# Loading the second expert's weights after the main loop instead of inside it

## The chip, the core and the metric

The kernel runs on one core of a Trainium2 chip. A core has five engines that take their instructions in order, each from its own stream: TensorE (PE, matrix products; its weight loads are listed as PEld), VectorE (DVE), ScalarE (ACT), GpSimd (POOL) and SyncE (SP, which here issues most DMAs). Sixteen DMA engines move data between the main memory (HBM) and the core's on-chip memory (SBUF); PE writes to a small accumulator memory (PSUM). The metric is the device time of one execution in microseconds (us), given as the median of several runs.

## What is computed

Three layers follow each other: masked attention, a dense layer with a softplus, and a mixture of eight experts in which each token takes at most one expert.

```python
# attention: q, k, v are (4, 8, 576, 64); keys of later blocks of 64 are masked
scores = np.where(mask, scale * q @ k.T, -1e9)
attn = exp(scores - max) / (sum(exp) + 1e-9);  x = (attn @ v) as (2304, 512)
# dense layer, 512 -> 2048 -> 512, in float32
h = x @ w_in;  x = softplus(h) @ w_out
# mixture of experts, E = 8, 512 -> 1024 -> 512
do_compute = x @ w_skip > 0;  out = x.copy()
xc = x[do_compute]
e_idx = argmax(xc @ w_gate, axis=1);  gate_w = softmax(xc @ w_gate)[e_idx]
for e in range(E):
    mask = e_idx == e
    if mask.any():
        y[mask] = gate_w[mask, None] * (relu(xc[mask] @ w1[e]) @ w2[e])
out[do_compute] = xc + y
```

One expert has two weight matrices of 2 MB each (w1: 512 x 1024, w2: 1024 x 512, float32). Which experts are needed, and for which tokens, is only known once the dense layer has produced those tokens.

## The kernel before

**Main loop.** After the attention, a loop of 80 steps (and 2 to drain) computes the dense layer. The 2304 tokens are cut into five chunks, numbered 0 to 4 here: four of 512 tokens and a last one of 256. The loop goes through the hidden columns in four groups and inside each group through the chunks, so that in the last group the chunks become final one after the other. Step `s` holds `layer1` (L570), `softplus` (L581 to L591) and, two steps late, `layer2` (L622). When a chunk is final, `close_unit` adds up its tiles (DVE, L633) and SP stores each tile twice: to a scratch copy `xd`, from which expert rows are gathered later, and to the output (L641).

**Routing, step by step beside the loop.** For each finished chunk, `transpose_x2`, `logits`, `route` and `append` find each token's expert and its place in that expert's list. The results `si` and `pay` are ready with the reciprocal of L746 on DVE; then `scatter` (L753) has POOL write them to the lists `lst` in HBM, 128 tokens in each scatter. A chunk of 512 tokens takes four scatters, the last chunk two. Each scatter waits until the scatter before it has landed, since they all write `lst`.

**Expert order.** After chunk 1, `rank_experts` ranks the experts by the number of tokens seen so far; the number of the largest (rank 0, the first expert) and of the next (rank 1, the second expert) are read by SP from a small table `tab` (`value_load`, L907). After chunk 2 the rest are ranked. `load_expert(r, b, part)` (L904 to L917) issues an expert's weights as eight DMAs of 512 KB on SP: parts 0 to 3 are w1 (L910), parts 4 to 7 are w2 (L915). They go to pages that the dense layer has finished with. SP's DMAs use eight semaphores in turn, so that each of them first waits for the landing of the one that stands eight before it.

**Early tiles.** For ranks 0 and 1 the first 128 listed tokens of chunks 0 to 2 are computed early: `early_lists` loads the two lists (L920, `idxe`) after the scatters of chunk 2; `early_rows` gathers the tokens' rows from `xd` (POOL, L923); `early_turn` transposes them (PE, L949; copy on DVE, L951); `early_l1` and `early_l2` (L964, L976) are the two products. The calls stand in the code behind the loop, woven with the routing of the last chunk.

**The rest.** The tokens that are left, here few for each of ranks 0 to 2, are computed together in `side_by_side`. Its rows come over the same path: lists complete (last scatter), `late_rows` loads the list pieces (L1000, `idxf`), gathers the rows (L923, `xgf`), `turn` transposes them (L1035), and then come L1576, L1587, L1600, L1610 and the last store (L928). In PE's order the transposes of L1035 stand in front of the last quarter of the second expert's early product.

The order of everything above is written out in the program. Steps of the routing are put at loop steps by `later(c, n, ...)`: n steps after the step in which chunk c is computed for the last time.

Of the kernel before, what the change touches and what calls it, by code (L numbers as in the profile page):

```python
# [22 lines left out]
def attention_softplus_moe_kernel(  # L23
# [13 lines left out]
    nc = tc.nc  # L37
# [3 lines left out]
    E, _, F = w1.shape  # L41
# [24 lines left out]
    tab = const.tile([1, 4, E], I32, name="tab")  # L66
    MAXF = (NT - 2 * P) // P
    further = const.tile([1, 3, MAXF], I32, name="further")
# [587 lines left out]
    def logits(c, t):  # L656

        if t == 0:
            lgs[c] = ps_r.tile([P, 512], F32, tag="lg", name="lg")
        if c >= last - 1 and t % 2:  # L660
            ps = ps_r.tile([P, P], F32, tag="tr", name="lq")
        else:
            ps = lgs[c][:, 256 + t % 2 * P:256 + (t % 2 + 1) * P]
        xt = x2T.pop((c, t))
        for kc in range(KC):
            nc.tensor.matmul(
                out=ps[32 * kc:32 * (kc + 1), :], lhsT=wg[:, kc, :], rhs=xt[:, kc, :], start=True, stop=True,
                tile_position=(0, 32 * kc),
            )
        lq = x2T[c, t] = rt_p.tile([P, P], F32, tag="lq", name="lq")  # L670
        nc.scalar.activation(out=lq, in_=ps, func=AF.Copy)
# [209 lines left out]
    def expert_page(b, j):  # L881

        if (b, j) not in pages:
            i = j - KC
            pages[b, j] = (
                x_page((0, 2, 3)[b], j) if i < 0 else x_page(1, i) if b == 0 else slot(2 * b + i // 2, "io"[i % 2])
            )
        return pages[b, j]

    def expert_w1(b, kc, f):  # L890

        return expert_page(b, kc).rearrange("p h c -> p (h c)")[:, f]
# [8 lines left out]
    NPART = KC + KF // 2  # L901
    expert_at = {}

    def load_expert(r, b, part):  # L904

        if part == 0 and r != "further":
            expert_at[r] = nc.sync.value_load(tab[0:1, int(r > 1), r:r + 1], min_val=0, max_val=E - 1)  # L907
        e = bass.ds(expert_at[r], 1)
        if part < KC:
            nc.sync.dma_start(  # L910
                out=expert_w1(b, part, slice(0, F)), in_=w1[e, part * P:(part + 1) * P, :].rearrange("o p f -> p (o f)")
            )
            return
        kf = 2 * (part - KC)
        nc.sync.dma_start(  # L915
            out=expert_page(b, part), in_=w2[e, kf * P:(kf + 2) * P, :].rearrange("o (h p) d -> p (o h) d", p=P)
        )  # L917

    def load_list(idx, s0):
        nc.sync.dma_start(out=idx, in_=lst[bass.ds(s0, P), :])  # L920
# [12 lines left out]
    early = {}  # L933

    def early_lists(a):
        idx = const.tile([P, 2], I32, name=f"idxe{a}")
        load_list(idx, expert_at[a] * STRIDE)
        early[a] = [idx]
# [16 lines left out]
    def early_l1(a, quarter):  # L955
        xgT, hT = early[a][2:4]
        half, odd = divmod(quarter, 2)
        if not odd:
            early[a, "pf"] = ps_h.tile([P, KF // 2, P], F32, tag="h", name="pfe")
        pf = early[a, "pf"]  # L960
        for f in range(odd * KF // 4, (odd + 1) * KF // 4):
            ff = half * (KF // 2) + f
            for kc in range(KC):
                nc.tensor.matmul(  # L964
                    out=pf[:, f, :], lhsT=expert_w1(a, kc, slice(ff * P, (ff + 1) * P)), rhs=xgT[:, kc, :],
                    start=(kc == 0), stop=(kc == KC - 1),
                )
        if odd:
            nc.scalar.activation(out=hT[:, half * (KF // 2):(half + 1) * (KF // 2), :], in_=pf, func=AF.Relu)
# [17 lines left out]
    def later(c, n, do, *args):  # L987

        routing_work.setdefault(after[c] + n, []).append(lambda: do(*args))
# [164 lines left out]
    later(1, 5, rank_experts)  # L1154
    for i in range(NPART):
        later(1, 6 + i // 4, load_expert, 0, 0, i)
        later(1, 8 + i // 4, load_expert, 1, 1, i)
    later(2, 5, rank_experts, True)
    later(2, 5, list_starts)
    for a in range(2):  # L1160
        later(2, 6, early_lists, a)
        later(2, 7, early_rows, a)
# [248 lines left out]
    for kc in range(KC):  # L1411
        for c, of in enumerate((X0, X1)):
            a, b = of[2 * kc], of[2 * kc + 1]
# [72 lines left out]
    for t in range(nt):  # L1486
        transpose_x2(last, t)
    early_l1(0, 1)
    for i in range(NPART):
        load_expert(2, 2, i)  # L1490
    logits(last, 0)
    early_l1(0, 2)
    logits(last, 1)
# [190 lines left out]
```

## Time and profile before

| | |
|---|---|
| time, median of 3 runs | 715.69 us (714.16 to 717.24) |
| the profiled execution's own time | 716.66 us |
| its span, first to last instruction | 714.9 us |
| PE busy | 681.4 us (95%) |
| DVE, ACT, POOL busy | 478.7, 369.1, 163.7 us |
| DMA | 57.78 MB, mean 81 GB/s |

PE is busy for 95% of the span, but the share says nothing of a single stage. The page's strip of 40 slices (17.9 us each) shows where the rest is:

```profile
PE   8999999999999999999999999999999999986996
PEclk9999999999999999999999999999999999997999
DMA  7536344342210111011011010100003041984520
GB/s 177 126 81 152 85 103 100 85 110 70 62 51 29 43 46 39 22 59 60 30 34 54 30 60 30 59 30 31 0 1 118 2 118 48 348 299 138 214 77 10
```

Each digit is a share in tenths; PEclk is the granted clock of TensorE. The slices 35 and 36 (607 to 643 us) hold the loads of the first two experts, slice 38 (661 to 679 us) that of the third. In slice 37 (643 to 661 us) PE is busy for 6 tenths and its clock is below full.

### The profile page before, as it was taken

To read this page: it belongs to the slowest core of one execution; us is meant where nothing else is said; L and a number is where in the kernel's file an instruction comes from. 1 tells how busy PE (TensorE), PEld (TensorE's weight loads), DVE (VectorE), ACT (ScalarE), POOL (GpSimd) and SP (SyncE) were. 2 spreads that over 40 slices of the span, in tenths; PEclk is the share of its full clock that TensorE was granted. 3 is DMA by queue.
4 is the path that set the end of the run, shared out by engine and by line. 5 is a ranking of instruction groups with operands and counts; after the bars stand their busy time and mean duration, and the time that the engine had idled before them with its cause. 6 is when DMAs were issued, how large, how long until landed. Compare 5 with 4: busy or idle time off the path is not lost. (4 is left out here: it accounts for less than half of the span.)

```text
span 714.9 us, 11536 instructions
## 1 busy us (share of the span) xinstructions
PE 681.4 (95%) x4164; PEld 525.9 (74%) x4164; DVE 478.7 (67%) x951; ACT 369.1 (52%) x884; POOL 163.7 (23%) x180
## 2 busy tenths in 40 slices
PE   8999999999999999999999999999999999986996
PEld 6677676776767888888888888888888777765742
DVE  4787787877898985677656688657765465473322
ACT  4887887878776655455444454444433323220111
POOL 2122121212266452122111122221110021113120
PEclk9999999999999999999999999999999999997999
DMA  7536344342210111011011010100003041984520
GB/s 177 126 81 152 85 103 100 85 110 70 62 51 29 43 46 39 22 59 60 30 34 54 30 60 30 59 30 31 0 1 118 2 118 48 348 299 138 214 77 10
DMA packets 88739, 57.78 MB, mean 81 GB/s; under 512 B 67391, under 2 KB 76607, under 8 KB 88674
## 3 DMA queue, kind: packets, MB, share of 16 engines
q1 hardware_dynamic: 86034, 54.40, 26.2%
q0 software_dynamic: 1296, 2.24, 1.1%
q8 instruction: 34, 0.56, 0.3%
q10 hardware_dynamic: 1344, 0.33, 0.2%
q14 instruction: 31, 0.25, 0.1%
HBM read 46.16 MB, written 10.92 MB: 80 GB/s over the span
## 5 line engine op out<-in xcount | busy, mean ns | idle before, releaser
L570 PE MATMUL h<-xs,wi 128*128 128x512 f32 (+1 forms) x960 | 215.6, 373 | 0.4 <-DVE xs L551 0.4
L570 PEld LDWEIGHTS h<-xs,wi 128*128 128x128 f32 x960 | 168.6, 188 | 36.7 <-issue 0.8
L622 PE MATMUL o<-wo,gh 128*128 128x512 f32 x576 | 183.0, 398 | 0.3 <-DVE wo L559 0.3
L622 PEld LDWEIGHTS o<-wo,gh 128*128 128x128 f32 x576 | 106.3, 188 | 24.0 <-DVE wo L559 0.8
L585 DVE SCALAR_TENSOR_TENSOR e<-h,e 128x512 f32<-128x512 f32 (+1 forms) x80 | 50.8, 635 | 105.0 <-ACT e L583 104.5
L622 PE MATMUL o<-wo,gl 128*128 128x512 f32 x288 | 114.2, 397 | 0.0
L581 ACT ACTIVATE e<-h 128x512 f32<-128x512 f32 (+1 forms) x80 | 44.1, 551 | 132.9 <-PE h L570 132.9
L268 POOL TENSOR_TENSOR cc<-cc,cb 128x512 f32<-128x512 f32 (+1 forms) x40 | 43.4, 1086 | 262.0 <-DVE cb L266 191.5
L412 ACT ACTIVATE p<-s,mx 128x128 f32<-128x128 f32 (+2 forms) x144 | 79.2, 554 | 35.9 <-DVE mx L394 18.9
L437 PE MATMUL tp<-ident,p 128*128 128x128 f32 x384 | 61.2, 284 | 12.1 <-ACT pt L463 9.1
L591 DVE TENSOR_TENSOR gl<-e,gh 128x512 fp32r<-128x512 f32 (+1 forms) x80 | 64.3, 804 | 6.5
L622 PEld LDWEIGHTS o<-wo,gl 128*128 128x128 f32 x288 | 54.2, 188 | 13.1
L437 PEld LDWEIGHTS tp<-ident,p 128*128 128x128 f32 x384 | 42.3, 141 | 21.4 <-ACT pt L463 13.0
L399 DVE TENSOR_REDUCE mx<-s 128x2 f32<-128x256 f32 (+1 forms) x64 | 50.9, 819 | 10.3 <-PE s L388 9.1
L481 PE MATMUL v<-pt,vr 128*64 128x320 f32 (+4 forms) x448 | 50.3, 364 | 0.0
L590 DVE CAST gh<-e 128x512 fp32r<-128x512 f32 (+1 forms) x80 | 44.2, 553 | 6.7 <-DVE e L585 0.5
L583 ACT ACTIVATE e<-e 128x512 f32<-128x512 f32 (+1 forms) x80 | 47.2, 590 | 2.5
L582 ACT ACTIVATE e<-e 128x512 f32<-128x512 f32 (+1 forms) x80 | 47.2, 589 | 2.5
L753 POOL DMA_INDIRECT lst<-pay,si x18 | 17.7, 985 | 128.6 <-DVE pay L746 80.5
L463 ACT ACTIVATE pt<-tp 128x512 f32<-128x512 f32 (+1 forms) x80 | 44.3, 558 | 3.0 <-PE tp L437 2.2
L481 PEld LDWEIGHTS v<-pt,vr 128*64 128x64 f32 x448 | 29.4, 136 | 20.3 <-issue 5.2
L260 ACT ACTIVATE cc<-raw 128x512 f32<-128x512 uint32 (+1 forms) x40 | 23.1, 578 | 25.6 <-POOL ca L269 25.5
(242 smaller groups left out, 942.5 us busy)
## 6 DMA issues: line engine op xcount, KB each, us to landing
xs<-in_moe_w_dram SPq DMA_DIRECT2D x16, 512.0 KB, 6.6
raw<-in_moe_w_in_dram SPq DMA_DIRECT2D x12, 512.0 KB, 3.7
raw<-in_moe_w_out_dram SPq DMA_DIRECT2D x12, 512.0 KB, 3.2
xd<-xT SPq DMA_DIRECT2D x18, 256.0 KB, 3.4
out_dram<-xT SPq DMA_DIRECT2D x18, 256.0 KB, 4.1
vr<-in_v_dram SPq DMA_DIRECT2D x32, 128.0 KB, 3.2
qr<-in_q_dram SPq DMA_DIRECT2D x30, 128.0 KB, 2.6
kr<-in_k_dram SPq DMA_DIRECT2D x30, 128.0 KB, 2.8
```

What stands on the lines that cost most here:

```text
L399: nc.vector.tensor_reduce(out=mx[:, c:c + 2], in_=ps[:, :, columns(t)], axis=AX.X, op=ALU.max, negate=True)
L412: nc.scalar.activation(out=y, in_=x, func=AF.Exp, bias=mx[:, c:c + 1], accum_out=sums[p][:, 0, 2 * t + h:2 * t + h + 1])
L437: nc.tensor.transpose(ps[:, at:at + P], pn[t, g][:, j * P:(j + 1) * P], ident)
L463: nc.scalar.activation(out=dst, in_=x, func=AF.Copy)
L481: nc.tensor.matmul(out=ps[h * D:(h + 1) * D, c0 - q0:q1 - q0], lhsT=vt[:, kt, h, :], rhs=rhs, start=(kt == 0), stop=(kt == nk - 1), skip_g ...
L570: nc.tensor.matmul(out=ps[:, 0:n], lhsT=a[:, kc, :], rhs=b[:, 0:n], start=(kc == 0 and j == 0), stop=(kc == KC - 1 and j == 2),)
L582: nc.scalar.activation(out=e[:, 0:n], in_=e[:, 0:n], func=AF.Exp, scale=-1.0)
L583: nc.scalar.activation(out=e[:, 0:n], in_=e[:, 0:n], func=AF.Ln, bias=1.0)
L585: nc.vector.scalar_tensor_tensor(out=g[:, 0:n], in0=ps[:, 0:n], scalar=0.0, in1=e[:, 0:n], op0=ALU.max, op1=ALU.add)
L590: nc.vector.tensor_copy(out=gh[:, 0:n], in_=g[:, 0:n])
L591: nc.vector.tensor_tensor(out=gl[:, 0:n], in0=g[:, 0:n], in1=gh[:, 0:n].bitcast(F32), op=ALU.subtract)
L622: nc.tensor.matmul(out=acc[c, t], lhsT=a[:, ts], rhs=b, start=(fc == f0 and j == 0), stop=(fc == f1 - 1 and j == 2),)
```

## The change

The eight loads of the second expert (rank 1) leave the steps at which chunk 3 is finished and go behind the main loop, directly in front of the third expert's. Since `early_lists(1)` still needs that expert's number, it now reads it itself, and `load_expert` does not read it again.

```diff
     def load_expert(r, b, part):
 
-        if part == 0 and r != "further":
+        if part == 0 and r not in expert_at and r != "further":
             expert_at[r] = nc.sync.value_load(tab[0:1, int(r > 1), r:r + 1], min_val=0, max_val=E - 1)
...
     def early_lists(a):
+        if a not in expert_at:
+            expert_at[a] = nc.sync.value_load(tab[0:1, int(a > 1), a:a + 1], min_val=0, max_val=E - 1)
         idx = const.tile([P, 2], I32, name=f"idxe{a}")
         load_list(idx, expert_at[a] * STRIDE)
...
     for i in range(NPART):
         later(1, 6 + i // 4, load_expert, 0, 0, i)
-        later(1, 8 + i // 4, load_expert, 1, 1, i)
...
     early_l1(0, 1)
-    for i in range(NPART):
-        load_expert(2, 2, i)
+    for r in (1, 2):
+        for i in range(NPART):
+            load_expert(r, r, i)
     logits(last, 0)
```

Only SP's stream is reordered; the instructions of PE, DVE, ACT and POOL stand in the same order as before, with line numbers two higher. In SP's stream of before, from the end of the first expert's loads to the lists of the early tiles, w1 of the second expert (`xs_6656` to `xs_6662`) stands ahead of chunk 3's eight stores and its w2 (`wi_6752` to `wo_6758`) behind them:

```order
L907 TENSOR_LOAD tab_65
...
L910 DMA xs_6656<-in_moe2_w1_dram 128x1024
...
L910 DMA xs_6662<-in_moe2_w1_dram 128x1024
L641 DMA xd_79<-xT_59 128x512
L641 DMA out_dram<-xT_59 128x512
...
L915 DMA wi_6752<-in_moe2_w2_dram 128x2x512
...
L915 DMA wo_6758<-in_moe2_w2_dram 128x2x512
L920 ISA
L920 DMA idxe0_6828<-lst_80 128x2
```

In the changed stream nothing but chunk 3's stores stands in front of the first list, and the read of the table stands between the two lists (L937):

```order
L915 DMA xs_6586<-in_moe2_w2_dram 128x2x512
L641 DMA xd_79<-xT_59 128x512
L641 DMA out_dram<-xT_59 128x512
...
L920 ISA
L920 DMA idxe0_6803<-lst_80 128x2
L937 TENSOR_LOAD tab_65
...
L920 DMA idxe1_6814<-lst_80 128x2
```

Further on in the changed stream, from the last chunk's stores to the list pieces of the rest, the second expert's loads (`xs_7000` to `wo_7014`) stand ahead of the third's (`xs_7025` to `wo_7039`), where before the third's stood alone:

```order
L641 DMA out_dram<-xT_59 256x1x256
L910 ISA
L910 DMA xs_7000<-in_moe2_w1_dram 128x1024
...
L915 DMA wo_7014<-in_moe2_w2_dram 128x2x512
L907 TENSOR_LOAD tab_65
...
L910 DMA xs_7025<-in_moe2_w1_dram 128x1024
...
L915 DMA wo_7039<-in_moe2_w2_dram 128x2x512
L1001 TENSOR_LOAD tab_65
...
L1002 DMA idxf_7143<-lst_80 64x2
```

So 4 MB move from beside chunk 3 to a place between the last chunk's stores and the list pieces, and 16 loads instead of 8 stand in front of those pieces.

## Rows read from the trace of the kernel before

**Rows 1.** Timeline of PE behind the main loop: start, duration (us), instruction, idle time before.
```profile
652.56 1.11 PE L949 MATMUL pxe<-ident,xT 128*128 128x128 f32 x4 [3.30 <-DMA xT<-xd,idxe]
654.46 3.78 PE L964 MATMUL pfe<-xT,xs 128*128 128x128 f32 x16 [0.78 <-DVE xT L951]
...
659.26 1.95 PE L964 MATMUL pfe<-xT,xs 128*128 128x128 f32 x16
```

**Rows 2.** Timeline of SP's DMA issues in the last 100 us.
```profile
616.32 3.29 SPq L910 DMA_DIRECT2D xs<-in_moe_w_dram  x4
...
635.53 0.48 SPq L915 DMA_DIRECT2D wi<-in_moe_w_dram  x1
...
646.70 0.89 SPq L920 DMA_DIRECT2D idxe<-lst  x2
654.10 0.59 SPq L641 DMA_DIRECT2D xd<-xT  x1
...
656.06 0.62 SPq L641 DMA_DIRECT2D out_dram<-xT  x1
658.42 2.25 SPq L910 DMA_DIRECT2D xs<-in_moe_w_dram  x4
...
676.80 3.14 SPq L1000 DMA_DIRECT2D idxf<-lst  x3
```

**Rows 3.** Timeline of POOL in the same stretch: scatters (L753) and gathers (L923).
```profile
629.32 0.97 POOL L753 DMA_INDIRECT lst<-pay,si  x1 [13.65 <-DVE pay L746]
...
636.65 0.97 POOL L753 DMA_INDIRECT lst<-pay,si  x1 [4.02 <-DMA lst<-pay,si]
643.79 0.97 POOL L753 DMA_INDIRECT lst<-pay,si  x1 [6.17 <-DMA lst<-pay,si]
649.28 0.98 POOL L923 DMA_INDIRECT xT<-xd,idxe  x1 [4.52 <-PE o L622]
...
651.83 1.01 POOL L753 DMA_INDIRECT lst<-pay,si  x1 [0.30 <-issue]
...
659.68 0.97 POOL L753 DMA_INDIRECT lst<-pay,si  x1 [1.53 <-DMA lst<-pay,si]
672.31 0.97 POOL L753 DMA_INDIRECT lst<-pay,si  x1 [11.66 <-DVE nums L810]
674.69 0.97 POOL L753 DMA_INDIRECT lst<-pay,si  x1 [1.41 <-DMA lst<-pay,si]
...
682.15 0.98 POOL L923 DMA_INDIRECT xgf<-xd,idxf  x1 [5.21 <-DMA idxf<-lst]
```

**Rows 4.** SP's own waits from 596 us on: total, times, longest (us).
```profile
SPq L920 <- DMA lst<-pay,si: 8.6, 1, 8.6
SPq L641 <- DMA xT<-xd,idxe: 6.4, 1, 6.4
```

**Rows 5.** Timeline of DVE: end of a chunk's routing (L746), closing of the last chunk.
```profile
649.11 0.18 DVE L746 RECIPROCAL pay<-se 128x4 f32<-128x4 f32 x1
649.20 1.26 DVE L633 TENSOR_TENSOR xT<-o,xT 128x512 f32<-128x512 f32 x2
...
671.87 0.17 DVE L746 RECIPROCAL pay<-se 128x2 f32<-128x2 f32 x1
```

**Rows 6.** Scatter issued at 659.68 us: issue to landing.
```profile
DMA to landing us min/median/max: 5.9/5.9/5.9
```

**Rows 7.** Stretch of the third expert's load: busy time by engine, clock, DMA share, GB/s.
```profile
658.40:671.30 12.90, 12.90 (x96) 9.73 (x95) 4.27 (x18) 1.86 (x5) 0.97 (x1) 0.99 0.92 331
```

**Rows 8.** Timeline of PE: second expert's first product, transposes of the rest.
```profile
673.69 7.31 PE L964 MATMUL pfe<-xT,xs 128*128 128x128 f32 x64
...
686.39 0.60 PE L1035 MATMUL pxl<-ident,xgf 128*128 128x128 f32 x4
```

**Rows 9.** Tile `xgf`, the gathered rows of the rest: its gather's time to landing.
```profile
DMA to landing us min/median/max: 3.9/3.9/3.9
```

**Rows 10.** Stretch behind the main loop: the clock is the third number from the end.
```profile
656.00:658.00 2.00, 2.00 (x11) 2.00 (x11) 0.00 (x0) 0.00 (x0) 0.81 (x1) 0.50 0.90 298
```

## The prediction, written before the change was timed

> **What bounds the kernel now.** I read the strip of 40 slices first: PE is full up to the end of the main loop, so only the last 70 us can change, and there I went through the timelines of PE, SP, POOL and DVE side by side, then SP's own waits. Three things are to be seen.
>
> First, PE stands still once. The loop's last product ends at 652.56 - 3.30 = 649.26, and the early tile's transposes wait 3.30 us for the gather of its rows [rows 1]. Backwards from there: the gather is issued at 649.28 [rows 3], its list is loaded by SP at 646.70 [rows 2], and SP had waited 8.6 us for the last scatter of chunk 2 [rows 4]. (The name PE that POOL's row gives as releaser of the gather is an old semaphore; what comes just before it is the list.) Those four scatters start at 629.32; the first two take 7.3 us together, the third, from 636.65 to 643.79, 7.1 us [rows 3]. The second expert's w2 is issued at 635.53 and the three issues after it, beside that scatter [rows 2]. With the DMA engines free a scatter takes 674.69 - 672.31 = 2.4 us [rows 3].
>
> Second, TensorE's clock falls around this halt to the lower level: the stretch from 656 to 658 us has a granted clock of 0.50, 1.2 GHz [rows 10]. Sixteen products of the early tile take 3.78 us there against 1.95 us once the clock is back [rows 1].
>
> Third, at the very end a chain without slack decides: last scatter of the last chunk, list pieces at 676.80 [rows 2], gather of the rest issued at 682.15 [rows 3], landed 3.9 us later, at 686.05 [rows 9], transposes on PE at 686.39 [rows 8]. PE was busy until then, so the chain is only 0.3 us ahead of being what PE waits for. This is where the change must be judged.
>
> **The part that is taken away.** No load of the second expert runs between 616 and 646 us any more. In the loop PE waits for none of it, so the loop ends at 649.26 as before. The scatters of chunk 2 become shorter: the first two stay as they are (their company is chunk 3's stores, which remain), the third starts at 636.65; third and fourth cost at least 2 x 2.4 (they end at 641.4) and at most what they cost now (646.7). I take 642, near the free value, since the stores were issued from 631 to 635 and a few of their bytes are left. From the list's issue to the rows on PE it takes 652.56 - 646.70 = 5.9 us [rows 1, 2], so the rows are there at 647.9, 1.4 us ahead of PE. What is late next is DVE: closing the last chunk keeps it until 649.20 + 1.26 = 650.46 [rows 5], and the early copy stands behind that. From the transposes' end to the first product it was 0.8 us [rows 1], so the product starts at about 651.2 instead of 654.46: PE is 3.25 us ahead. If the scatters of chunk 2 ended later than 643.4, each us would be lost again, up to all 3.25.
>
> I count nothing for the clock here. It was full again after some 5 us of work at the lower level (1.11 and 3.78 us, and a little behind them [rows 1]); the same work would bring it back again. What that cost is 3.78 - 1.95 = 1.8 us for the products [rows 1], 1.11 - 0.60 = 0.5 for the early transposes against the like of them in [rows 8], and some 0.4 for the last chunk's transposes between 658.2 and 659.3: 2.7 us. In the best case all of it is saved.
>
> The read of the table now stands between the two lists. Its like, in front of the third expert, fills the gap between the last store's issue and the first load, 658.42 - 656.68 = 1.7 us [rows 2]. It delays the second early list and so the last chunk's stores, which wait for both gathers [rows 4]; there they meet DVE at 650.46 anyway, so I count nothing, 1 us at most.
>
> **The part that is added.** The last chunk's four stores start near 650.4 instead of 654.10 and take 2.6 us to issue [rows 2]; the first load of the second expert follows at about 653 instead of the third's at 658.42. Eight loads took 12.9 us at 331 GB/s [rows 7]; sixteen take 25 to 26 us, so the DMA engines are full from 653 to about 678.5, where before they were full from 658.4 to 671.3.
>
> The weights themselves are in time. The second expert's w1 is half of the first eight loads and lands by 662 to 666; its product is due at 673.69 - 3.25 = 670.4 [rows 8]. The third expert's w1 lands by about 673, and its product comes after the transposes of the rest, later than 683. I count nothing.
>
> The scatters are not. Six of them fall into this stretch: chunk 3's four and the last chunk's two, each waiting for the one before. A scatter that starts beside such loads is bounded below by 2.4 us (the free one) and above by 7.1 us; the two that ran beside loads took 7.1 [rows 3] and, at 659.68, 5.9 to landing and some 6.2 to the next issue [rows 6]. I take 7.1, since the queue of 16 loads is deeper than the one beside either. The chain:
> - chunk 3's first: its data are ready at 649.29 [rows 5], so it runs from 649.6 (POOL issued it at 651.83 before [rows 3]) to 652.0;
> - the second starts ahead of the loads and ends among them: between 2.4 and 7.1 us, I take 4.7, to 656.7;
> - third and fourth: 7.1 each, to 663.8 and 670.9;
> - the last chunk's first: its data were ready at 672.04 [rows 5], now at 668.8; it starts at 671 and takes 7.1, to 678.1;
> - its second: the loads are just over, 2.4 us, to 680.5.
>
> Before, the list pieces were issued at 676.80, so the last scatter comes 3.7 us later, though PE is 3.25 us earlier. From the list pieces to the landed rows it is 686.05 - 676.80 = 9.25 us, hence 689.75. PE reaches its transposes at 686.39 - 3.25 = 683.1 and halts 6.6 us. They start 689.8 - 686.39 = 3.4 us later than before. Behind the waiting transposes stands the last quarter of the second expert's early product, and everything of `side_by_side` after it; no other work fills the gap.
>
> A halt of 6.6 us is twice the one that went with the fall of the clock before. So I charge the same loss again, 2.7 us; its bounds are 0 and, if the lower level lasts twice as long, 5.4 us. From there to the end nothing changes.
>
> **Sum.** 3.4 + 2.7 = 6.1 us more than the profiled execution's 716.66 (its span of 714.9 and 1.8 around it). That execution is 1.0 us above the median of the runs; I add the difference to the median: 715.69 + 6.1 = 721.8 us. With 6.2 us for a scatter beside loads and 2.4 for the second one, the last of them ends at 678.5 and the sum is +1.4 without a loss of the clock, +4.1 with it. With 7.1 for the second one too, and the loss doubled, it is 5.3 + 5.4 = +10.7. So the forecast's own range is 717 to 726.4.
>
> **Rivals.**
> - *The scatters stay short* (not slower). If a scatter beside the loads took the free 2.4 us, the last would land at 668.8 + 0.3 + 4.8 = 673.9, the rows of the rest at 683.1, just when PE wants them, and the 3.25 us in front stay: 712.4 us. It decides at 3.25 us a scatter for the four that meet the loads fully or in part, if the loads also end by 671; otherwise it is the last chunk's two alone that decide. For it: the first two scatters of chunk 2 took 3.7 us each on average beside other DMAs [rows 3]. Against it: the rows of 7.1 and 5.9 us, both beside eight or fewer loads. The Trainium skill, "DMA: Bandwidth & Descriptors", section "Queues, rings and completion order", says that each DMA engine takes turns between the queues it has work for, packet by packet; by that a scatter's few short packets would not wait behind all queued loads, and the time would come out near this rival's 712.4. The trace has a scatter three times as long as a free one, so it bears the rule out only in part.
> - *The clock is kept as well* (faster). With the 3.30 us of halt gone, the clock might stay up or come back at once: 2.7 us more, with short scatters 715.69 - 3.25 - 2.7 = 709.7. Against it: a wait of DVE for the last chunk is left in the place of the halt (650.46 to 651.2), and the work needed to bring the clock back is the same.
> - *Half way* (no difference). The scatters are slowed, but the chain ends around 677.5 because the loads are over sooner (at a rate 10% above that of [rows 7] sixteen would take 23 us): rows at 686.8, +0.4, and some of the clock: 716 to 719.
> - *The weights come late* (slower still). If the third expert's w1 were not there for its product, which comes behind the transposes, PE would wait once more. With the forecast's transposes at 689.8 the first twelve loads would have to last 37 us, 6.3 MB at 170 GB/s; nothing in [rows 7] speaks for it. With the short scatters of the first rival they would be due behind 683, still 10 us after they land. A chain that is longer because a scatter takes 9 us instead of 7.1 is likelier: four times 1.9 more, 727 to 730.
>
> **Chances.** Forecast, all of it slower by over 0.5% but for its lower end: 0.62. Half way: 0.16. Short scatters: 0.11. Clock kept as well: 0.05. Slower than my range: 0.06. A measurement of this kernel can tell about 0.5%, 3.6 us, from no change: faster is below 712.1, slower above 719.3. The short scatters' 712.4 lies on that line, so a third of them counts as faster: faster 0.09. Same gets the rest of them (0.07), half way (0.15) and the forecast's lower end (0.06): 0.28. Slower 0.63. For the time I leave out the two outer cases in part: 713.0 to 726.0.
>
> **What would show it.** Right in front: SP issues the first list near 642 instead of 646.70, PE's transposes of the early tile have no wait for the gather, and the first early product starts near 651. Right in the middle: POOL's scatters after 652 are 6 to 7 us apart instead of 2.4, and the last chunk's first starts when the one before has landed, not when DVE is ready. Right at the end: PE waits 5 to 8 us ahead of L1035's transposes (two lines lower in the changed kernel) for the gather of the rest, and the granted clock shows a second stretch of 0.50 there. I am wrong if scatters beside sixteen loads take under 4 us; if PE waits for a weight load; or if the early tile still waits, which would leave only the loss.

## The result, and the profile after

The changed kernel takes 722.98 us (median of 4 runs, 722.59 to 724.31), the one before 715.16 beside it (4 runs, 714.16 to 717.24): a ratio of 1.0116, 95% interval 1.0092 to 1.0141. It is slower by 7.8 us; the forecast was 721.8.

The profiled execution takes 722.59 us, with a span of 720.9; before it was 716.66. These 5.93 us lie in two places, and both can be read from POOL and PE. First PE's timeline of the changed kernel, for the rows of [rows 1] and [rows 8]; lines stand two further down than before (L949 is L951, L1035 is L1037).

```profile
649.49 0.60 PE L951 MATMUL pxe<-ident,xT 128*128 128x128 f32 x4
651.78 2.05 PE L966 MATMUL pfe<-xT,xs 128*128 128x128 f32 x16 [1.70 <-DVE xT L953]
...
668.97 7.31 PE L966 MATMUL pfe<-xT,xs 128*128 128x128 f32 x64
...
690.06 1.08 PE L1037 MATMUL pxl<-ident,xgf 128*128 128x128 f32 x4 [8.22 <-DMA xgf<-xd,idxf]
690.94 3.62 PE L978 MATMUL pye<-wo,hTe 128*128 128x512 f32 x4
```

The early tile's transposes wait for nothing now (3.30 us before), and the second expert's first product starts at 668.97 instead of 673.69: in front PE is 4.7 us ahead. At the end it stands still for 8.22 us until the rows of the rest are there, and its transposes start at 690.06 instead of 686.39, 3.67 us later. What made the rows late is on POOL, in the rows that answer to [rows 3]:

```profile
638.33 0.97 POOL L753 DMA_INDIRECT lst<-pay,si  x1 [2.70 <-DMA lst<-pay,si]
644.33 0.98 POOL L923 DMA_INDIRECT xT<-xd,idxe  x1 [5.03 <-PE lq L666]
...
650.24 1.00 POOL L753 DMA_INDIRECT lst<-pay,si  x1 [3.66 <-DVE pay L746]
654.04 1.00 POOL L753 DMA_INDIRECT lst<-pay,si  x1 [2.80 <-DMA lst<-pay,si]
660.39 0.97 POOL L753 DMA_INDIRECT lst<-pay,si  x1 [5.35 <-DMA lst<-pay,si]
666.20 0.97 POOL L753 DMA_INDIRECT lst<-pay,si  x1 [4.85 <-DMA lst<-pay,si]
672.58 0.97 POOL L753 DMA_INDIRECT lst<-pay,si  x1 [5.41 <-DVE nums L810]
678.03 0.97 POOL L753 DMA_INDIRECT lst<-pay,si  x1 [4.48 <-DMA wo<-in_moe_w_dram]
...
686.59 0.98 POOL L923 DMA_INDIRECT xgf<-xd,idxf  x1 [6.31 <-DMA idxf<-lst]
...
716.24 1.00 POOL L928 DMA_INDIRECT out_dram<-wo,idxf  x1 [18.46 <-POOLq L1638]
```

From the second scatter of chunk 3 (654.04) to the last one (678.03) each step takes 5.4 to 6.4 us, against 2.4 between the last chunk's two in [rows 3]. The weights are what runs beside them. SP's issues, for those of [rows 2], and the stretch of the loads, for [rows 7] (busy time of PE, PEld, DVE, ACT, POOL, then clock, DMA share, GB/s):

```profile
641.75 1.49 SPq L920 DMA_DIRECT2D idxe<-lst  x2
...
653.41 2.25 SPq L910 DMA_DIRECT2D xs<-in_moe_w_dram  x4
...
658.86 4.47 SPq L910 DMA_DIRECT2D xs<-in_moe_w_dram  x4
...
668.46 0.37 SPq L915 DMA_DIRECT2D wo<-in_moe_w_dram  x1
680.83 3.55 SPq L1002 DMA_DIRECT2D idxf<-lst  x3
```
```profile
653.00:678.50 25.50, 25.33 (x178) 19.54 (x177) 7.58 (x38) 3.05 (x7) 4.38 (x5) 1.00 0.98 358
```

The DMA engines are full over 25.5 us, and four of the six scatters (those from 654.04 to 672.58) run beside the loads; the list pieces come at 680.83 instead of 676.80. The clock is the second place. It is full where [rows 10] had 0.50, and at the lower level around the halt of the tail. In front it wasn't kept either: a short stretch at the lower level lies earlier, inside the main loop, from 636 to 640 us:

```profile
636.00:640.00 4.00, 4.00 (x31) 3.24 (x25) 1.93 (x4) 0.28 (x1) 0.97 (x1) 0.58 0.27 88
656.00:658.00 2.00, 2.00 (x24) 1.68 (x22) 0.00 (x0) 0.77 (x2) 0.00 (x0) 1.00 0.99 352
684.00:694.00 10.00, 3.94 (x8) 1.91 (x8) 0.69 (x1) 0.00 (x0) 3.83 (x4) 0.52 0.38 108
```

From the transposes to the last store's issue it takes 716.24 - 690.06 = 26.18 us; in the trace of before 710.31 - 686.39 = 23.92, the last store standing in this row:

```profile
710.31 1.00 POOL L928 DMA_INDIRECT out_dram<-wo,idxf  x1 [16.42 <-POOLq L1636]
```

So 3.67 us for the later rows and 2.26 for the clock make 5.93, all of the difference between the two executions.

### The profile page after: what moved, and what is told of

It is laid out like the page before. It is cut to its first block, busy times and chain, and to the rows that moved or that the text cites. A ratio compares the mean times of both kernels' runs of the same rounds, so it can differ in the third digit from the quotient of the medians.

```text
span 720.9 us, 11537 instructions
## 1 busy us (share of the span) xinstructions
PE 680.8 (94%) x4164; PEld 524.2 (73%) x4164; DVE 478.5 (66%) x951; ACT 369.1 (51%) x884; POOL 163.7 (23%) x180
## 5 line engine op out<-in xcount | busy, mean ns | idle before, releaser
L753 POOL DMA_INDIRECT lst<-pay,si x18 | 17.7, 985 | 132.2 <-DVE pay L746 83.6
L260 ACT ACTIVATE cc<-raw 128x512 f32<-128x512 uint32 (+1 forms) x40 | 23.0, 576 | 25.6 <-POOL ca L269 25.5
```

## The experiments

Theory A, the prediction's: the price comes from the scatters that run beside weight loads, and from the clock that falls in the halt which follows. Rival B: the wait that the trace shows newly on DVE. The index tile `si` of the routing has one buffer, so the last chunk's copy into it has to wait for chunk 3's last scatter:

```profile
671.59 0.17 DVE L740 CAST si<-s 128x2 int32<-128x2 f32 x1 [4.99 <-DMA lst<-pay,si]
...
672.22 0.13 DVE L810 TENSOR_TENSOR nums<-base,nums 1x8 f32<-1x8 f32 x1
```

The kernel before was run beside each set: 715.22, 716.48 and 715.40 us (13, 15 and 29 runs).

**Without the second expert's loads.** Its products read the first expert's pages, so its weights are left out.

```
-    for r in (1, 2):
-        for i in range(NPART):
-            load_expert(r, r, i)
+    for i in range(NPART):
+        load_expert(2, 2, i)
...
     def expert_page(b, j):
+        b = 0 if b == 1 else b
```

> The changed kernel without the second expert's eight loads (its product uses the first expert's pages, so its tokens get the wrong weights). Theory A, the scatters beside the loads are the price: eight loads are left behind the loop, over near 666 us. Chunk 3's second and third scatter stay slow (6 us), its fourth and the last chunk's two become 2.4 to 3 us, so the list pieces are issued near 674.5 instead of 680.8, PE's halt ahead of the transposes of the rest shrinks from 8.2 to about 2 us, the clock is kept: 8 to 9 us less than the changed kernel, about 714. Rival B, the price is the copy of the places (L740), which waits on DVE for the scatter before: it would still wait, 2 us less at most. Rival C, the reordered list reads cost the time: no change, 722.

Measured: 716.62 us, ratio 1.0015 (0.9992 to 1.0037). Eight of the sixteen loads are worth about 1% (722.98 against 716.62 us). But with the second expert loaded nowhere, in front or behind, the kernel is still not faster than before. POOL's timeline shows why:

```profile
654.00 1.00 POOL L753 DMA_INDIRECT lst<-pay,si  x1 [2.75 <-DMA lst<-pay,si]
658.26 0.97 POOL L753 DMA_INDIRECT lst<-pay,si  x1 [3.26 <-DMA lst<-pay,si]
664.85 0.97 POOL L753 DMA_INDIRECT lst<-pay,si  x1 [5.62 <-DMA lst<-pay,si]
671.12 0.97 POOL L753 DMA_INDIRECT lst<-pay,si  x1 [5.30 <-DVE nums L810]
673.49 0.97 POOL L753 DMA_INDIRECT lst<-pay,si  x1 [1.41 <-DMA lst<-pay,si]
```

The loop's shorter end brings the third expert's loads forward too, to 654.2 from 658.42 [rows 2]. Now the second scatter of chunk 3 meets them in part and the third and fourth go beside them (4.26, 6.59 and 6.27 us to the next), where before it was the fourth alone, and the last one comes at 673.49, only 1.2 us earlier than in [rows 3]. PE then halts 3.37 us in the tail, and the clock falls there (0.52 from 684 to 688 us); theory A had 714 us, a halt of 2 us and the clock kept. So the gain in front is given back by the loads that follow it.

**The kernel before, with the third expert loaded twice.** Eight loads more behind the loop, and nothing moved in front of them.

```
-    for i in range(NPART):
-        load_expert(2, 2, i)
+    for _ in range(2):
+        for i in range(NPART):
+            load_expert(2, 2, i)
```

> The kernel before, with the third expert's eight loads issued twice in a row; all loads of the second expert stay where they were. Theory A: sixteen loads run from 658 to about 683, the scatters from 660 on take 5 to 6 us each, the list pieces are issued near 683 instead of 676.8, PE halts 6 us ahead of the transposes of the rest and the clock falls there: 8 us more than before, about 724. Rival C (the place of the second expert's loads or of the list reads matters, not the traffic): no change, 716. Rival D, weights late: PE would wait on a weight load of the third expert, the halt on the gather would be short.

Measured: 721.43 us, ratio 1.0106 (1.0069 to 1.0142). This is nearly all that the change costs (1.0116), from the eight loads alone, though less than the 724 us that A had. Here they catch the last chunk's two scatters and what stands behind them:

```profile
668.85 0.97 POOL L753 DMA_INDIRECT lst<-pay,si  x1 [9.12 <-DVE nums L810]
674.43 0.97 POOL L753 DMA_INDIRECT lst<-pay,si  x1 [4.61 <-DMA lst<-pay,si]
...
685.34 0.98 POOL L923 DMA_INDIRECT xgf<-xd,idxf  x1 [8.66 <-DMA idxf<-lst]
```

5.58 us from the first to the second (2.4 in [rows 3]), and the gather at 685.34 instead of 682.15. This execution is ahead of the one of [rows 8] in front (the second expert's first product at 670.23, there 673.69), so the second scatter goes no later than in [rows 3]; it lands 5.8 us later, and the list pieces follow at 680.25 instead of 676.80.

**Two buffers for `si` and `pay`** in the changed kernel.

```
-            return rt_p.tile([P, *shape], dtype, tag=nm, name=nm, bufs=1)
+            return rt_p.tile([P, *shape], dtype, tag=nm, name=nm, bufs=2 if nm in ("si", "pay") else 1)
```

> The changed kernel with two buffers for the places and their payload (si, pay), so that DVE writes those of the last chunk without waiting for chunk 3's last scatter. Theory A: the scatters follow each other anyway; the last chunk's first starts 0.3 us behind the landing of the one before instead of 1.2: 0.5 to 0.9 us less, about 722. Rival B, DVE's wait of 5 us is what makes the chain late: 4 to 5 us less, 718.

Measured: 722.9 us, ratio 1.0111 (1.0081 to 1.0141), as the change itself. DVE's wait is gone: its copy into `si` runs at 667.30. The last chunk's first scatter goes 0.8 us after the landing of the one before (665.74 + 5.4 = 671.14, issue at 671.91) instead of 1.2 (666.20 + 5.2 = 671.40, issue at 672.58):

```profile
665.74 0.97 POOL L753 DMA_INDIRECT lst<-pay,si  x1 [5.28 <-DMA lst<-pay,si]
671.91 0.97 POOL L753 DMA_INDIRECT lst<-pay,si  x1 [5.20 <-DVE nums L826]
677.49 0.97 POOL L753 DMA_INDIRECT lst<-pay,si  x1 [4.61 <-DMA lst<-pay,si]
```

B falls: the wait for the buffer was a wait for the same scatter. Taking it away shortens the step by 0.2 us (6.17 from 665.74, against 6.38 from 666.20) and shows nowhere in the times.

**TensorE kept busy in the halt of the tail**, first with 14 products.

```
     early_l2(1, 2)
+    idle = ps_r.tile([P, 512], F32, tag="tr", name="idle")
+    for _ in range(14):
+        nc.tensor.matmul(out=idle, lhsT=ident, rhs=expert_w1(0, 0, slice(0, 512)), start=True, stop=True)
```

> The changed kernel with 14 products of 128x512 whose result nobody reads, put on PE ahead of the transposes of the rest, 6.5 us of work in the halt of 8.2 us. The halt's end is set by the gather and stays at 690. If the lower clock behind the halt costs what its rows say (1.08 against 0.60 us and 3.62 against 1.88), 2.2 to 2.3 us less, about 720.5. Rival: the work behind the halt is bound by DVE and ACT and the clock costs nothing: no change.

Measured: 724.34 us, ratio 1.0132 (1.0103 to 1.0162). I had mis-sized the products: they took 12.18 us, 0.87 apiece, and pushed the transposes to 694.34. But the clock stayed full, and from there to the last store it took 718.25 - 694.34 = 23.91 us. With 8 products:

> The changed kernel with 8 products of 128x512 that nobody reads in PE's halt ahead of the transposes of the rest: 7.0 us at the 0.87 us apiece that the 14 of the run before took, so they end before the gather lands. If the lower clock behind the halt costs 2.3 us (from the transposes of the rest to the last store 23.9 us with filler, 26.2 without, in the profiles so far), 2.3 us less than the changed kernel: 720.7, and the granted clock stays at 1.00 behind the halt. Rival: the clock falls all the same, or the end is bound by DVE and ACT: no change, 723.

Measured: 719.52 us, ratio 1.0044 (1.0028 to 1.0060); the change itself had 1.0116. PE's and POOL's timelines:

```profile
681.67 7.03 PE L1527 MATMUL idle<-xs,ident 128*128 128x512 f32 x16
689.12 0.63 PE L1037 MATMUL pxl<-ident,xgf 128*128 128x128 f32 x4 [0.42 <-DMA xgf<-xd,idxf]
```
```profile
685.66 0.98 POOL L923 DMA_INDIRECT xgf<-xd,idxf  x1 [5.62 <-DMA idxf<-lst]
...
713.07 1.00 POOL L928 DMA_INDIRECT out_dram<-wo,idxf  x1 [15.76 <-POOLq L1641]
```

713.07 - 689.12 = 23.95 us, 2.23 less than in the changed kernel: this is the price of the clock. The other 0.9 us by which the profile is shorter come from a gather that was issued 0.93 us earlier; nothing in the edit explains these.

**Fewer loads behind the loop.** In the next ones the second expert's w1 is loaded in the main loop and only its w2 behind it, with all of the third (12 loads); or all of the second behind the loop and the third behind the gathers of the late rows (8 loads, then 8).

```
         later(1, 6 + i // 4, load_expert, 0, 0, i)
+        if i < KC:
+            later(1, 8, load_expert, 1, 1, i)
...
+    for i in range(KC, NPART):
+        load_expert(1, 1, i)
```

> Half the change: the second expert's w1 is loaded where it was before, only its w2 goes behind the loop, ahead of the third's eight loads. Theory A: twelve loads run from 653 to about 673; chunk 3's second to fourth scatter are slow (5 to 6 us), the last chunk's first partly, its second is free; list pieces near 678, halt of 5 to 6 us with the fall of the clock: about 720, between the changed kernel (723) and the one without the second's loads (716.6). Rival (all that matters is that loads stand there at all): 722 to 723.

Measured: 718.73 us, ratio 1.0039 (1.0025 to 1.0053). Three of chunk 3's scatters still go beside loads, the last chunk's two are short, the last one comes at 674.90, and the transposes start at 686.39, the same as before; from there it is 712.03 - 686.39 = 25.64 us, since the clock fell in a halt of 2.42 us.

> The changed kernel with the third expert's loads behind the list pieces and lists of the rest instead of behind the second's. Theory A: eight loads beside the scatters as in the kernel without the second expert's loads, so the list pieces go out near 675.5 and PE halts 3 to 4 us for the gather; the third's loads start near 681.5, beside that gather, which may land 1 to 2 us later, and its w1 is there by 690, just before its product: about 717. Rival D, weights late: PE waits 3 us or more for the third's w1, 720 or more.

Measured: 720.1 us, ratio 1.0048 (1.0029 to 1.0067). The last chunk's scatters are short again (669.63 and 672.01), yet the gather is issued only at 682.61, 10.6 us after the last one (7.46 in [rows 3]). The list pieces were issued at 674.12; from there to the gather it takes 8.49 us, and 7.13, 6.51 and 6.89 in the three runs below that also put loads behind the late rows, against 5.05 to 6.04 in the other nine traces. All of these loads are issued behind the gather, and the DMA engines are nearly free until then (a share of 0.10 from 676 to 680 us here), so it isn't the traffic of A. Why the stretch is longer stays open. The third expert's w1 is 0.25 us late for its product.

**Loads placed by hand into the pauses**: w1 in the loop; a read of the list, as a gate, behind chunk 3's last scatter, then the second's w2; all of the third behind the late rows' gathers.

```
+    load_list(const.tile([P, 2], I32, name="probe"), 0)
+    for i in range(KC, NPART):
+        load_expert(1, 1, i)
...
     late_rows()
+    for i in range(NPART):
+        load_expert(2, 2, i)
```

> A version built on theory A: the second expert's w1 is loaded where it was before; behind the loop SP first loads 1 KB of the lists into a scratch tile, which waits until chunk 3's last scatter has landed, then the second's w2 (four loads), then the list pieces and lists of the rest, and the third's eight loads only behind them. Theory A: the early tile keeps its earlier start (no halt for the gather in front), chunk 3's scatters run free from 650 to 660, w2 is loaded from 660 to 667, the last chunk's scatters follow free from 667.5, the list pieces go out near 672.5, the rows land near 682 to 683, beside the first loads of the third, and PE hardly halts: 712 to 713, 2 to 3 us under the kernel before. Rival D: the third's w1, issued from 678.5, comes after its product is due (688): 715 or more. If scatters are slow for another reason than the loads: 718 or more.

Measured: 717.12 us, ratio 1.0024 (1.0007 to 1.0042): about 0.9% better than the change, no better than before, a miss. Chunk 3's scatters have no loads beside them any more (647.38 to 657.15, steps of 3.3, 2.4 and 4.0 us), but w2 meets the last chunk's first scatter, 4.30 us to the next, and the third expert's loads meet the gather: from the gather at 678.28 to the transposes at 683.32 it is 5.04 us, 0.8 more than before (686.39 - 682.15 = 4.24). Then the clock falls, and the w1 product waits 0.62 us.

The same with second's w2 and third's w1 right behind the loop and only the third's w2 behind the late rows:

> Second's w1 in the main loop, second's w2 and third's w1 right behind it (8 loads, about 13 us), third's w2 behind the gathers of the late rows. Theory A (the scatters that go beside loads set the list): the loads end near 664, so two of chunk 3's four scatters are loaded (about 5.5 us apiece) and both of the last chunk's are short (2.1 to 2.4 us from one to the next). Against the run with 12 loads there, whose last scatter was given at 674.9 and whose transposes began at 686.4, the last scatter comes near 671 and the transposes near 682.5; the weights that TensorE asks for next (third's w1) are there, so no wait for weights follows. Time 714 to 716 us, 0.997 to 1.000 of before. Rival B (a load moved behind the list costs the gathers as much as it cost the scatters): the four loads of third's w2 lie beside the gather of the full rows, the transposes begin near 685.5, and the time is 717 to 719 us.

Measured: 718.81 us, ratio 1.0029 (1.0010 to 1.0047). The last scatters are short, as A says (670.02 and 672.39, the last one 1.4 us later than expected). But the transposes start at 686.34; rival B of this run had 685.5. The gather of the rows now goes beside w2, and its time to landing is, here and in the run with 12 loads, where it goes alone:

```profile
DMA to landing us min/median/max: 5.2/5.2/5.2
```
```profile
DMA to landing us min/median/max: 3.3/3.3/3.3
```

The load that was moved behind the list slowed the next small transfer, here by 1.9 us. The size varies: in the next run, where the same four loads start 1.2 us behind the gather, it takes 4.4 us, and 3.3 to 3.9 in the traces that time it without loads.

The same with four products in the tail's halt (the edit of above, with 4):

> As e7_split, with four products of 128x512 (eight instructions, about 3.5 us) on TensorE in the halt of the tail. Theory A: the granted clock doesn't fall behind the halt, and from the transposes to the last store it takes 23.9 us (26.2 at the lower clock); so 1 to 2.3 us less than e7_split, 712 to 714 us, 0.994 to 0.997 of before. Rival C (where the clock is kept in the tail it falls elsewhere in the same execution): the stretch is 23.9 us here too, but the time is that of e7_split, and the mean clock of the execution is no higher than there.

Measured: 716.58 us, ratio 1.0030 (1.0007 to 1.0053). The tail's 23.95 us are there (684.75 to 708.70 in the profile), but the ratio is that of the run without the products; the medians are 2.2 us apart and the runs of both are spread over 5.3 and 8.5 us. Theory A had 712 to 714 us. Rival C is not borne out in its second sign: over the 12 runs of each the mean granted clock is 0.994 with the products and 0.991 without, so the clock isn't lost elsewhere. Yet the mean times are 717.4 and 717.8 us; why the kept clock doesn't show in them stays open.

**Four such products in the kernel before.**

> The kernel before with four such products in its own halt ahead of the transposes (3.3 us there). Theory A: before's profiled execution kept its clock in the tail, so these products buy nothing in such an execution, and cost nothing; in others the fall may come in the tail. 714 to 716 us, 0.997 to 1.000 of before. Rival C: 715 to 717 us, no difference. Rival D (the products delay the transposes, since they are queued ahead of them): 717 us or more.

Measured: 718.37 us, ratio 1.0046 (1.0028 to 1.0065): slower. I had misread the halt, too: the 3.3 us are those in front [rows 1], and ahead of L1035 the kernel before hardly waits. In this execution the gather was issued at 679.41, and PE was not free to use it:

```profile
682.60 3.60 PE L1525 MATMUL idle<-xs,ident 128*128 128x512 f32 x8
686.03 0.60 PE L1035 MATMUL pxl<-ident,xgf 128*128 128x128 f32 x4
```

From the gather's issue to PE it was 4.24 us before (686.39 - 682.15) and 3.47 after the change (690.06 - 686.59), so the transposes could have started at 683 to 683.7; they start behind the products, without a wait. This is rival D: work put into a halt costs when the halt isn't there. It is read from this one execution; the median of 718.37 fits its 717 or more.

No version beat the kernel before.

## Why the prediction was right

The time, the sign and the places are as forecast. Step by step:

- *The front.* The list is issued at 641.75 (forecast: near 642), and the transposes of the early tile have no wait. The first product starts at 651.78, 0.6 us later than forecast, because DVE's part of the loop's end ran from 649.87 instead of 649.20. Its 16 products take 2.05 us, not 3.78: the clock is full there, since its low stretch lies in the loop this time (636 to 640, shown above). By the second expert's product the lead is 4.7 us, where I had 3.25; how much of it is the change's, see the base below. The read of the table that I put at 1.7 us costs 0.6: the two lists' issues take 1.49 us with it between them and 0.89 before. Nothing hung on it.
- *The loads.* Full from 653 to 676 and over by 678.5, as forecast; PE waits for no weight.
- *The scatters.* The list pieces are issued at 680.83, forecast 680.5. This is closer than the terms behind it, and by luck: from one scatter to the next I had 2.4, 4.7, 7.1, 7.1, 7.1, measured are 3.8, 6.35, 5.81, 6.38, 5.45. A scatter beside loads costs about 6 us here and not 7.1, and the second of chunk 3 is fully beside them; the two errors cancel. My reason for 7.1, that a deeper queue costs more, isn't borne out: beside eight loads it was 6.59 and 6.27.
- *From the list to PE.* 690.06 - 680.83 = 9.23 us, forecast 9.25. PE halts 8.2 us, forecast 6.6, since it came earlier.
- *The clock.* The fall in the tail costs 2.26 us, forecast 2.7; shown by taking it away (2.23). With the clock full the stretch is 23.91, 23.95 and 23.95 us in the three runs that put such products into a halt of the tail, 23.92 before.
- *The base.* The two profiled executions differ by 5.93 us, the medians by 7.8. I added the sum to the median, as if the execution that I read were like the rest. But the kernel before does not always lose its clock in this place: the run of it with four products is the same program up to 682 us, and there the lower level came some 12 us earlier. Windows of before, then of that run (the clock is the third number from the end), and that run's PE behind the loop:

```profile
636.00:640.00 4.00, 3.56 (x36) 2.92 (x37) 2.73 (x6) 0.89 (x4) 0.97 (x1) 1.00 0.99 268
648.00:652.00 4.00, 1.26 (x5) 0.45 (x3) 2.28 (x11) 0.00 (x0) 2.11 (x3) 0.56 0.25 67
```
```profile
636.00:640.00 4.00, 4.00 (x33) 3.18 (x26) 2.04 (x5) 0.35 (x2) 0.00 (x0) 0.61 0.99 269
648.00:652.00 4.00, 2.34 (x18) 1.49 (x14) 2.83 (x14) 0.00 (x0) 2.88 (x3) 1.00 0.44 131
```
```profile
651.21 0.66 PE L949 MATMUL pxe<-ident,xT 128*128 128x128 f32 x4 [1.52 <-DMA xT<-xd,idxe]
652.65 2.05 PE L964 MATMUL pfe<-xT,xs 128*128 128x128 f32 x16 [0.78 <-DVE xT L951]
...
669.84 6.41 PE L964 MATMUL pfe<-xT,xs 128*128 128x128 f32 x56
```

  The early products take 2.05 us here without the change, and the second expert's first comes at 669.84: the change is 0.9 us ahead of this execution, not 4.7. The run with the third expert loaded twice, whose front is before's too, is of the same kind (0.64 from 636 to 640, 2.05 us, 670.23: 1.3 us). So most of the front's gain, my 3.25 us, stood in the one trace that I read. The changed kernel's tail doesn't hang on it, since the rows and not PE decide there. But the kernel before, run like this, could have started its transposes near 683 (worked out above for the run with four products) and not at 686.39: in executions like this one the tail's price has less to set against it, which is how the medians can lie further apart than the two profiles. How often the kernel before runs the one way or the other isn't known: two of three traces with its front have the fall at 636, one at 648.

The rivals: *short scatters* fell with the rows on POOL, *half way* with the time; *the clock kept as well* was wrong: the clock fell at 636 us in the loop, ahead of the place that it spoke of, and again in the tail. *Weights late* didn't happen, and neither did scatters of 9 us.

## What to carry to other kernels

A bulk load that is taken off one chain of small dependent transfers falls on the next one: before moving it, count the scatters, list reads and gathers that lie under each place where it could go, at the price that they have beside a load. What is won ahead of a chain that decides the end also brings forward the loads issued behind it, and can be lost there whole. And read a second execution, if there is one, before adding a sum to a median: a loss that one trace shows may not be in the others.

## What the hardware showed that I had not expected

- A scatter of 128 list entries lands in 2.1 us when the DMA engines are free, and in 4.0 to 6.9 us where weight loads run beside most of it: 4.0, 6.3 and 5.1 with eight loads queued (the run without the second expert), 6.1, 5.5, 5.2 and 5.2 with sixteen (the changed kernel), and 6.9 in the kernel before at 636.65, beside four loads and chunk 3's stores. A deeper queue doesn't show as a longer landing. The times to landing of the last scatter of the run without the second expert, and of the one at 672.58 in the changed kernel:

```profile
DMA to landing us min/median/max: 2.1/2.1/2.1
```
```profile
DMA to landing us min/median/max: 5.2/5.2/5.2
```

  The Trainium skill, "DMA: Bandwidth & Descriptors", section "Queues, rings and completion order", says that a DMA engine alternates between its queues packet by packet. That the depth of the other queue doesn't show in the landings agrees with it; the 2 to 5 us that the loads add all the same were only to be had from the trace.
- The stretch at the lower clock moves between executions of the same instructions, from 636 to 640 us in one to 648 and later in another, as the windows above show. Of the thirteen traces, ten have it at 636 to 640 (a granted clock of 0.57 to 0.75 there), the changed kernel's among them.
